# Eighteen orders of reading the streamed operand, one for each wide block, in a kernel of linear attention and a softplus feed-forward layer

## The chip, the cores and the metric

The kernel runs on one core of one Trainium2 chip. Time is device time in microseconds (us) of one launch. The time before is the median of three runs. The profile is of one further execution, recorded by the hardware profiler.

## What is computed

```
# q, k, v: (8, 8, 576, 64); g_norm: (64,)
kv  = einsum('bhsd,bhse->bhde', k, v)
out = einsum('bhsd,bhde->bhse', q, kv)
rms = sqrt(mean(out * out, axis=-1, keepdims=True) + 1e-06)
x   = (out / rms * g_norm).transpose(0, 2, 1, 3).reshape(4608, 512)
# moe_w_in: (512, 2048); moe_w_out: (2048, 512)
h = x @ w_in
g = maximum(h, 0.0) + log1p(exp(-abs(h)))
result = g @ w_out                  # (4608, 512), float32
```

## The kernel before

Nearly all the work is the two large products of the feed-forward layer. Each of their operands is split into three parts of a reduced 32-bit type, and each product is three matrix products, of part 0 with part 0, 1 with 1 and 2 with 2, summed in PSUM. So one logical product of a 128 x 128 weight piece with a block of columns is three matmuls.

There are three phases over the hidden width of 2048, which is cut into 16 chunks of 128.

- Phase 0 also does the attention. It goes over the 4608 tokens in twelve blocks of 384 (`n`), with hidden chunks 0 to 3 for the first four blocks and 0 to 5 for the rest. `step` has `mm1` (L863: 384 streamed columns, read in order, 12 matmuls) and `mm2` (L870: 512 streamed columns, read in order, 3 matmuls a tile of 128 tokens).
- Phases 1 and 2 go over the tokens in nine wide blocks of 512 (`n` from 0 to 8), and take the remaining hidden chunks two at a time: a pair `p` is chunks 2p and 2p + 1. `PAIRS` (L251) gives the pairs of each block: three in every block of phase 1, and in phase 2 three in the first three blocks and two in the last six. `STEPS` (L252) is the list of (phase, block, pair), 45 in all; `wide_step` (L1043) is one of them.

The first product of a wide step, `x @ w_in` for 256 hidden units and 512 tokens, uses a form with seven products of half size in place of eight. `units_of` (L958) prepares from the loaded tokens the seven streamed operands `u` (tiles `units`, `early` and `turned`), and `both` (L553) prepares the four combinations of the weights. `product(u, q)` (L1058) is one of the seven products: for the three parts `m` and the two halves `kd` of its contraction one matmul each, six in all. Its stationary operand is a 128 x 128 piece of the weights, its streamed operand is 256 columns (`HW`, half of `WIDE`) of `dst`, and its output is 256 columns of PSUM, quarter `q` of the step's two banks (`place(q)`). Streamed operand and output both go through `from_the_end` (L42), which cuts the 256 columns into 16 blocks of 16 and goes over the blocks from the last to the first, with the columns inside a block in ascending order. The output is taken in the same order as the operand, so each column arrives at its own place.

Between the products ScalarE copies a quarter to another (L1107, L1111) and VectorE adds (L1115); softplus is taken on ScalarE (L1093 and `x2`, `x4`, `xd_` in `wide_step`), the result is split again (L1123, L1126, L1129), and `mm2` (L1136) multiplies it with `w_out`: for two chunks and four tiles of 128 tokens three matmuls each, 24 a step, with 512 streamed columns read in ascending order. `leave` (L912) takes the sums out of PSUM.

The order in which every engine issues its instructions is written by `Plan.order` (L95), a list scheduler that runs when the program is built. It is given an estimated duration and a due position for each task; a whole product of six matmuls is one task on the PE queue with 710 ns (L1074). With this, products of one step, `mm2` of the step before and the loads of later blocks are interleaved. The order is not affected by how a matmul's operands are addressed.

Of the kernel before, what the change touches and what calls it, by code (L numbers as in the profile page):

```python
# [18 lines left out]
P = 128  # L19
# [19 lines left out]
    return x.rearrange(f"r ({' '.join(names)}) -> r {' '.join(names)}", **dict(zip(names, shape[1:])))  # L39


def from_the_end(x):  # L42

    return x.rearrange("p (b w) -> p b w", w=16)[:, ::-1]


class Slot:
# [159 lines left out]
def kernel(  # L207
# [24 lines left out]
    nc = tc.nc  # L232
# [17 lines left out]
    n_wide = n_tokens // WIDE  # L250
# [127 lines left out]
    def halves(src, e):  # L378

        return src[e * NP:(e + 1) * NP].rearrange("p s d -> s p d")  # L380
# [662 lines left out]
    def wide_step(k):  # L1043
        ph, n, p = STEPS[k]
        ab, gv = slot("ab"), slot("gvp")
        b = starts[k]
# [6 lines left out]
        def place(q):  # L1053
            return ab.tile[:, q // 2, q % 2 * HW:(q % 2 + 1) * HW]
# [3 lines left out]
        def product(u, q):  # L1058
            f, i = PRODUCTS[u]
            w = forms[p][f].tile  # L1060
            dst, v = unit_slots[ph, n, u]
            for m in range(3):
                for kd in range(2):
                    at = i * 2 * P + kd * P
                    nc.tensor.matmul(from_the_end(place(q)), lhsT=w[:, m, at:at + P],  # L1065
                                     rhs=from_the_end(dst.tile[:, m, v, kd] if u < 6 else dst.tile[:, m, kd]),
                                     start=(u == 0 and not m and not kd), stop=(m == 2 and kd == 1), skip_group_check=True)

        def multiply(u, q, after, pos, take=(), follows=None):
            f = PRODUCTS[u][0]  # L1070
            give = [unit_slots[ph, n, u][0]] if last else []
            if final and u in (2, 3, 5, 6):
                give.append(forms[p][f])
            return add("PE", 710, lambda: product(u, q), unit_done[ph, n, u] + forms_done[p][f] + list(after), pos, take, give,  # L1074
                       follows=follows)
# [19 lines left out]
        def begin():  # L1095
            new(ab, None)
            product(0, X)
# [168 lines left out]
```

## Time and profile before

| | us |
|---|---|
| median of three runs | 866.85 |
| lowest, highest | 865.42, 867.55 |
| the profiled execution's own time | 868.08 |
| its span, first to last instruction | 866.2 |
| granted TensorE clock, mean | 0.998 of full |
| TensorE busy | 851.7 |
| VectorE busy | 704.5 |
| ScalarE busy | 520.8 |

TensorE's instructions by line, from the groups of the profile (a line's groups by source tile are added):

| line | what | matmuls | streamed columns |
|---|---|---|---|
| L863 | first product, phase 0 | 768 | 384 |
| L870 | second product, phase 0 | 576 | 512 |
| L1065 | the seven products, phases 1 and 2 | 2016 | 256 |
| L1136 | second product, phases 1 and 2 | 1152 | 512 |

The profile gives a matmul as an interval from its start to a modelled end. Matmuls are pipelined, so these intervals overlap and their mean length is more than the distance between two starts. The chain of waits follows the work that ended last back to its start, and its pieces of one line in a row give that distance: length over count. The first instruction of L1065 starts at 340.6 us, in the last stretch of phase 0, and the last at about 854; phases 1 and 2 fill the rest of the span. The last block ends with 39 matmuls of L1136 (8.92 us from 853.52), a scaling of the last tile and its store.

### The profile page before, as it was taken

How to read it: one execution, taken by the hardware profiler on the slowest of the kernel's cores; microseconds unless marked ns; L12 is line 12 of the kernel's file. 1: busy time of each engine (PE TensorE's matmuls, PEld its weight loads, DVE VectorE, ACT ScalarE, POOL GpSimd, SP SyncE). 2: the span in 40 equal slices, each digit the busy share in tenths (PEclk: the TensorE clock that was granted, in tenths of full speed). 3: DMA queues.
4: the chain of work that ended last, by engine and by line, in shares of the span. 5: the costliest groups of instructions: out<-in, count | busy, mean ns of one | idle time of the engine just before them, and what ended most of it. 6: DMA issues, size and time to landing. Idle time of an engine off the chain costs nothing.

```text
span 866.2 us, 17080 instructions
## 1 busy us (share of the span) xinstructions
PE 851.7 (98%) x6464; PEld 758.6 (88%) x6464; DVE 704.5 (81%) x995; ACT 520.8 (60%) x980; POOL 76.1 (9%) x79
## 2 busy tenths in 40 slices
PE   7899999999999999999999999999999999999998
PEld 5678888989898899998999998998999899999996
DVE  7888898888788889798888788878788766788873
ACT  5766565445344567776667665655868555566654
POOL 0351123111113300000000000000000000000000
PEclk9999999999999999999999999999999999999999
DMA  9998997778774655436645546645354653787764
GB/s 273 278 218 216 285 259 227 188 250 215 206 186 119 194 157 180 143 113 198 211 155 161 167 152 203 193 154 185 122 191 139 233 166 100 238 240 237 247 189 128
DMA packets 239778, 167.07 MB, mean 193 GB/s; under 512 B 106320, under 2 KB 198736, under 8 KB 239696
## 3 DMA queue, kind: packets, MB, share of 16 engines
q1 hardware_dynamic: 239392, 165.86, 64.8%
q8 instruction: 50, 0.82, 0.4%
q14 instruction: 32, 0.26, 0.1%
q10 hardware_dynamic: 304, 0.13, 0.1%
HBM read 112.98 MB, written 52.95 MB: 192 GB/s over the span
## 4 chain that ended last, share of the span: by engine, by line
PE 93%; DMA 3%; DVE 2%; ACT 1%; POOL 1%; SPq 0%; issue 0%; DVEq 0%; ACTq 0%
PE banks L1136 30%; PE banks L1065 28%; PE banks L870 15%; PE banks L863 15%; PE banks L720 2%; PE banks L696 2%; DMA loads<-in_v_dram 1%; DMA raw<-in_moe_w_in_dram 1%; PE banks L738 0%; PE banks L1230 0%; POOL roots L728 0%; DVE half L732 0%; SPq L766 0%; DVE units L643 0%; ACT w L802 0%
## 5 line engine op out<-in xcount | busy, mean ns | idle before, releaser
L1136 PE MATMUL banks<-pieces,gv 128*128 128x512 f32 x768 | 238.1, 391 | 0.0
L1136 PE MATMUL banks<-pieces,g_False 128*128 128x512 f32 x384 | 150.6, 392 | 0.0
L1136 PEld LDWEIGHTS banks<-pieces,gv 128*128 128x128 f32 x768 | 132.6, 188 | 17.8
L863 PE MATMUL banks<-units,pieces 128*128 128x384 f32 x768 | 145.4, 337 | 0.0
L870 PE MATMUL banks<-pieces,gv 128*128 128x512 f32 x576 | 144.9, 396 | 0.0
L863 PEld LDWEIGHTS banks<-units,pieces 128*128 128x128 f32 x768 | 135.5, 188 | 4.9
L870 PEld LDWEIGHTS banks<-pieces,gv 128*128 128x128 f32 x576 | 106.1, 188 | 20.4
L1065 PEld LDWEIGHTS banks<-units,pieces 128*128 128x128 f32 x840 | 112.0, 188 | 6.6 <-ACT banks L1111 0.4
L1065 PE MATMUL banks<-units,pieces 128*128 128x256 f32 x840 | 116.4, 282 | 0.0
L885 ACT ACTIVATE half<-banks 128x384 f32<-128x384 f32 x64 | 31.5, 491 | 97.8 <-PE banks L863 97.7
L1126 DVE TENSOR_TENSOR gv<-g_True,gv 128x1024 fp32r<-128x1024 f32 x47 | 57.5, 1223 | 37.2 <-ACT gv L1123 37.2
L1136 PEld LDWEIGHTS banks<-pieces,g_False 128*128 128x128 f32 x384 | 71.9, 187 | 16.5
L1065 PEld LDWEIGHTS banks<-units,w 128*128 128x128 f32 x504 | 67.3, 188 | 3.8 <-ACT banks L1111 0.2
L1065 PE MATMUL banks<-units,w 128*128 128x256 f32 x504 | 70.3, 282 | 0.0
L728 POOL TENSOR_TENSOR roots<-roots,half 128x8 f32<-128x8 f32 x36 | 62.0, 1722 | 3.0
L1129 DVE SCALAR_TENSOR_TENSOR g_False<-gv 128x1024 fp32r<-128x1024 f32 x47 | 57.6, 1225 | 1.5
L1028 DVE TENSOR_TENSOR units<-loads,units 128x1024 fp32r<-128x1024 f32 x42 | 51.2, 1219 | 6.3 <-ACT units L1025 6.3
L1115 DVE TENSOR_TENSOR g_True<-banks,g_True 128x512 f32<-128x512 f32 x48 | 33.1, 691 | 28.4 <-PE banks L1065 23.1
L1093 ACT ACTIVATE g_True<-banks 128x256 f32<-128x256 f32 x96 | 36.7, 383 | 31.8 <-PE banks L1065 31.2
L930 ACT ACTIVATE m<-banks 128x512 f32<-128x512 f32 x72 | 42.1, 596 | 18.5 <-PE banks L1136 12.9
L1031 DVE SCALAR_TENSOR_TENSOR units<-units 128x1024 fp32r<-128x1024 f32 x42 | 51.4, 1223 | 1.8
L1025 ACT ACTIVATE units<-loads 128x1024 fp32r<-128x1024 f32 x42 | 44.4, 1057 | 13.4 <-PE banks L1065 10.4
(115 smaller groups left out, 1252.0 us busy)
## 6 DMA issues: line engine op xcount, KB each, us to landing
loads<-x SPq DMA_DIRECT2D x180, 128.0 KB, 2.7
part<-m SPq DMA_DIRECT2D x72, 256.0 KB, 2.8
m<-part SPq DMA_DIRECT2D x72, 256.0 KB, 3.3
loads<-form SPq DMA_DIRECT2D x45, 256.0 KB, 3.2
form<-loads SPq DMA_DIRECT2D x36, 256.0 KB, 2.9
raw<-in_moe_w_in_dram SPq DMA_DIRECT2D x16, 512.0 KB, 4.6
loads<-in_k_dram SPq DMA_DIRECT2D x32, 256.0 KB, 4.3
loads<-in_v_dram SPq DMA_DIRECT2D x32, 256.0 KB, 4.6
```

What stands on the lines that cost most here:

```text
L728: nc.gpsimd.tensor_tensor(out=r.tile, in0=r.tile, in1=half, op=ALU.pow)
L863: nc.tensor.matmul(hp, lhsT=w_in.tile[:, i, kd * P:(kd + 1) * P], rhs=xv.tile[:, i, kd], start=(m == 0), stop=(m == 3 * KD - 1))
L870: nc.tensor.matmul(mine[i].tile, lhsT=gv.tile[:, m, i * P:(i + 1) * P], rhs=w_out.tile[:, m], start=(c == cs[0] and m == 0), stop=(c == cs ...
L930: a = add("ACT", 690 if ph == LAST else 600, lambda: nc.scalar.activation(new(ot, [P, d_model]), bank.tile, func=AF.Copy, scale=scale if p ...
L1025: nc.scalar.activation(part_of(0, F32R), xl.tile if m > 1 else xl.tile[:, 0], func=AF.Copy, scale=DOWN)
L1028: nc.vector.tensor_tensor(out=part_of(1, F32R), in0=xl.tile if m > 1 else xl.tile[:, 0], in1=part_of(0), op=ALU.subtract)
L1031: nc.vector.scalar_tensor_tensor(out=part_of(2, F32R), in0=part_of(1), scalar=-RADIX, in1=part_of(0), op0=ALU.mult, op1=ALU.add)
L1065: nc.tensor.matmul(from_the_end(place(q)), lhsT=w[:, m, at:at + P], rhs=from_the_end(dst.tile[:, m, v, kd] if u < 6 else dst.tile[:, m, kd ...
L1093: nc.scalar.activation(dst, src, func=AF.Softplus, scale=1.0 + E)
L1126: nc.vector.tensor_tensor(out=gvt(1, F32R), in0=gt(), in1=gvt(0), op=ALU.subtract)
L1129: nc.vector.scalar_tensor_tensor(out=gt(F32R), in0=gvt(1), scalar=-RADIX, in1=gvt(0), op0=ALU.mult, op1=ALU.add)
L1136: nc.tensor.matmul(mine[i].tile, lhsT=(gvt(m, F32R) if m < 2 else gt(F32R))[:, c, i * P:(i + 1) * P], rhs=outs[c].tile[:, m], start=fresh ...
```

## The change: one order for each wide block

`from_the_end` is replaced by `in_order(x, k)`, which has eighteen ways to go over the 256 columns. `k` is 0 to 8 for the wide blocks of phase 1 and 9 to 17 for those of phase 2. All matmuls of the seven products of a block use its order, for the streamed operand and for the output alike, so the same numbers arrive at the same places.

```diff
-def from_the_end(x):
-
-    return x.rearrange("p (b w) -> p b w", w=16)[:, ::-1]
+def in_order(x, k):
+
+    def blocks(w):
+        return x.rearrange("p (b w) -> p b w", w=w)
+
+    def halves(w):
+        return x.rearrange("p (e j w) -> p j e w", e=2, w=w)
+
+    def quarters(w):
+        return x.rearrange("p (e j w) -> p j e w", e=4, w=w)
+
+    def inside(e, w):
+        return x.rearrange("p (b e w) -> p b e w", e=e, w=w)
+
+    return [lambda: x,
+            lambda: blocks(16)[:, ::-1],
+            lambda: blocks(8)[:, ::-1],
+            lambda: blocks(4)[:, ::-1],
+            lambda: blocks(32)[:, ::-1],
+            lambda: blocks(64)[:, ::-1],
+            lambda: blocks(2)[:, ::-1],
+            lambda: halves(16)[:, ::-1],
+            lambda: inside(8, 16)[:, :, ::-1],
+            lambda: inside(4, 16)[:, :, ::-1],
+            lambda: quarters(16)[:, ::-1, ::-1],
+            lambda: quarters(4),
+            lambda: quarters(8),
+            lambda: halves(16)[:, ::-1, ::-1],
+            lambda: inside(2, 16)[:, :, ::-1],
+            lambda: inside(4, 8)[:, :, ::-1],
+            lambda: inside(4, 4)[:, :, ::-1],
+            lambda: x[:, ::-1]][k]()
...
-                    nc.tensor.matmul(from_the_end(place(q)), lhsT=w[:, m, at:at + P],
-                                     rhs=from_the_end(dst.tile[:, m, v, kd] if u < 6 else dst.tile[:, m, kd]),
+                    k = n_wide * (ph - 1) + n
+                    nc.tensor.matmul(in_order(place(q), k), lhsT=w[:, m, at:at + P],
+                                     rhs=in_order(dst.tile[:, m, v, kd] if u < 6 else dst.tile[:, m, kd], k),
```

In words, by the number of the order:

- 0: ascending, one run of 256 columns.
- 1: blocks of 16 columns from the last to the first, as before. 2, 3, 4, 5 and 6: the same with blocks of 8, 4, 32, 64 and 2.
- 7: the halves in turn, a run of 16 from each, from the end of both. 13: the same, with the upper half first.
- 8, 9 and 14: groups of 8, 4 and 2 runs of 16; the groups ascend, and the runs inside a group go backward. 15 and 16: groups of 4 runs of 8 and of 4 columns, in the same way.
- 10: the quarters in turn, a run of 16 from each, from the end, with the last quarter first. 11 and 12: the quarters in turn, runs of 4 and of 8, ascending.
- 17: every single column from the last to the first.

## The prediction

> **What bounds the kernel now.** I read the page first, for the busy shares, then the chain of waits, for who sets the end, then the waits of the changed line, and last the chain in order of time, for the pitch of its matmuls.
>
> ```profile
> span 866.2 us, 17080 instructions
> PE 851.7 (98%) x6464; PEld 758.6 (88%) x6464; DVE 704.5 (81%) x995; ACT 520.8 (60%) x980; POOL 76.1 (9%) x79
> ...
> PE 93%; DMA 3%; DVE 2%; ACT 1%; POOL 1%; SPq 0%; issue 0%; DVEq 0%; ACTq 0%
> ...
> L1065 PE MATMUL banks<-units,pieces 128*128 128x256 f32 x840 | 116.4, 282 | 0.0
> ```
>
> TensorE is busy for 98% of the span and holds 93% of the chain that ended last. The row of L1065 (one of its five, by source tile) shows no idle time before its matmuls. Its mean of 282 ns is one matmul from its start to its modelled end; consecutive ones overlap, so it is not what one costs. The instructions of L1065 and their waits say how much slack stands in front of them:
>
> ```profile
> its engine sat idle before it (us, times) until:
>   ACT banks L1111: 0.6, 3
> ```
>
> 0.6 us in 2016 matmuls: a nanosecond more on one of them is a nanosecond more of span, and a nanosecond less is one less, as long as VectorE (339.7 us busy in the 420 us from 380 to 800) and ScalarE (262.5 us) keep up. The price of one matmul is its pitch, which the chain in order of time gives, as the length of an unbroken run over its count:
>
> ```profile
> 130.28 4.12 PE banks L870 x18
> 138.86 4.19 PE banks L863 x24
> ...
> 383.74 2.75 PE banks L1136 x12
> ...
> 485.61 2.84 PE banks L1065 x24
> ```
>
> L863 streams 384 columns: 4.19 / 24 = 174.6 ns. L870 and L1136 stream 512: 4.12 / 18 = 228.9 and 2.75 / 12 = 229.2 ns. L1065 streams 256 in reversed blocks of sixteen: 2.84 / 24 = 118.3 ns, and the same 2.84 stands in run after run, over several wide blocks. L863, L870 and L1136 read straight ahead.
>
> **The change.** Nothing is added or removed: the same 2016 matmuls, with the same loads, waits and buffers; no DMA, queue or wait moves. What changes is the order in which 256 columns are read from SBUF and, in the same order, accumulated in PSUM. Each wide block has one order: 3 steps of 7 products of 6 matmuls make 126 for the nine blocks of phase 1 and the first three of phase 2; the last six have 2 steps, 84. 12 x 126 + 6 x 84 = 2016. Order 1 is today's, so 1890 matmuls change.
>
> No row shows a 256-column matmul of L1065 read in another order. The bounds come from the neighbours. *Straight ahead:* the line through 384 and 512 columns falls by 229.2 - 174.6 = 54.6 ns for 128 columns and gives 120.0 ns at 256, 1.7 above today's. Pure proportion, with no fixed part, gives 174.6 x 256 / 384 = 116.4, 1.9 below. So any order of long runs lies, as a change, between -1.9 x 1890 = -3.6 us and +1.7 x 1890 = +3.2 us. *Orders of short runs* (two columns in order 6, single columns read backward in order 17, four in 3, 11 and 16): at worst each column takes two slots, and a 256-column matmul costs what a 512-column one does: 229.2 - 118.3 = +110.9 ns. At best nothing.
>
> I take these values. Orders 2 to 5, 7, 10 and 13 begin at or near the far end, as today's does: 0. Order 0 (126), 11 (126) and 12 (84) go upward: the full 1.7 ns, 336 x 1.7 = 0.57 us. Orders 8, 9, 14, 15 and 16 go backward only inside groups that go upward: half, (2 x 126 + 3 x 84) x 0.85 = 0.43 us. Orders 6 and 17: 0, because they still use every column of each small neighbourhood one after the other, and because today's fifteen jumps show no price: 118.3 lies below the 120.0 of the straight line. That is the weakest step; its upper ends are 126 x 110.9 = 14.0 us (order 6) and 84 x 110.9 = 9.3 us (order 17). Sum: +1.0 us.
>
> One more row makes small prices small: a weight load of L1065 takes 188 ns and runs beside the matmuls, with the weight row busy 379.5 of 420 us. No row tells whether the stream or the load sets the pitch of 118.3; if it is the load, an order a little slower is hidden behind it.
>
> A block that gets slower makes nothing else late: ScalarE already waits for L1065 (50.0 us at the copy of L1111, 31.2 at the softplus of L1093), and those waits only grow; SP's loads come earlier relative to their use. A block that gets faster meets the few waits on ScalarE first.
>
> The profiled execution took 868.08 us around its span of 866.2; the median of the three runs is 866.85. The sum is a difference, so on the profiled execution it gives 869.1 and on the median **867.9 us**, which I forecast.
>
> [...]
>
> **The rivals.**
>
> *Single columns backward are slow (slower).* [...] 84 x 110.9 = +9.3 us on top of the 1.0: 866.85 + 10.3 = 877.2. [...] Against it: the same neighbours are still read one right after another. [...]
>
> *Runs of two are slow as well.* Then order 6 costs 14.0 us: with order 17, 891.1; alone, 881.9. For it: 127 jumps against today's 15. [...]
>
> *Each jump has a small price.* Taking today's 118.3 as 116.4 plus fifteen jumps, a jump costs (118.3 - 116.4) / 15 = 0.127 ns. Orders differ from today's by -15 jumps (0), +16 (2, 12, 15), +48 (3, 11, 16), -8 (4), -12 (5) and +112 (6): over the 126 of the long blocks these add up to 126 x (-15 + 16 + 48 - 8 - 12 + 112 + 48) = 23814 jumps, over the 84 of the short ones 84 x (16 + 16 + 48) = 6720, together 3.9 us; with 240 more in order 17, 20160 jumps, 6.4 us. Time: 870.8 to 873.3. Against it: the straight line, by which jumps cost nothing.
>
> *Runs of four are slow too.* Orders 3, 11 and 16, 336 x 110.9 = +37.2 us: 928.4 with the others. Today's row says nothing of runs this short.
>
> *Today's order is a poor one (faster).* If the proportion holds and most orders reach 116.4, up to -3.6 us: 863.2, more likely half, 865.0. For it: proportion is the only lower bound there is. Against it: it leaves no fixed part, while the two widths show none either way.
>
> *The order does nothing at all,* since the weight load sets the pitch: 866.85. It is one case with the forecast.
>
> **How the numbers follow.** Chances: forecast 0.38, single columns slow 0.24, two columns slow 0.10 (0.03 of it without order 17), jumps priced 0.14, runs of four slow 0.06, faster 0.08. What a measurement of this kernel can tell from no change is about 0.3%, 2.6 us: 864.25 to 869.45. The forecast's own range, with the bounds of the long runs, is 863.5 to 870.1; of its 0.38, 0.30 fall within 0.3%, 0.06 above, 0.02 below. Jumps: 0.11 slower, 0.03 within. Faster: 0.06 and 0.02 within. Three cases of slow short runs: all 0.40 slower. Together faster 0.08, within 0.35, slower 0.57: the likeliest single case is within the bound, yet the slower cases together weigh more. The range has to take in the single-column case with the error of the long runs (877.2 + 3) and order 6 alone (881.9): 863.5 to 883.0. Left out are both short-run orders slow (0.07), runs of four (0.06) and the far end of faster (0.03), 0.16.
>
> **What would show it.** In the chain in order of time, runs of L1065 x24 of 2.8 to 2.9 us in every wide block say the forecast is right. A step now takes 42 x 118.3 + 24 x 229.2 ns = 10.5 us, the three-step block 31.4 and the last 20.9. If order 17 is slow, the last block takes 30.3 us and its runs of six 1.37 instead of 0.71; if order 6 is, the seventh block takes 45.4. If jumps are priced, the run of 24 grows in step with the count of jumps, most in order 6 (118.3 + 14.2 = 132.5 ns). Straight-ahead block 0 at 2.88 us for 24 would confirm the line, at 2.79 the proportion. A wait of L1065 above a few us in total, or other groups of instructions growing, would refute the claim that only the pitch matters. The forecast is wrong if any single block is over 2.6 us longer.

## The result, and the profile after

The changed kernel takes 871.24 us (median of four runs, 870.83 to 872.0) against 866.7 before (four runs, 865.42 to 867.55): 4.5 us more, ratio 1.0055 with a 95% interval of 1.0037 to 1.0072.

From the page of the changed kernel, where L1095 is the line of the seven products and L1166 that of the second product:

```profile
span 868.9 us, 17077 instructions
PE 855.7 (98%) x6464; PEld 762.4 (88%) x6464; DVE 704.8 (81%) x995; ACT 522.2 (60%) x980; POOL 76.0 (9%) x79
...
PE 94%; DVE 2%; DMA 2%; ACT 1%; POOL 1%; issue 0%; SPq 0%; DVEq 0%; ACTq 0%
...
L1095 PE MATMUL banks<-units,pieces 128*128 128x256 f32 x840 | 118.5, 284 | 0.0
```

TensorE still sets the end and still hardly waits before the changed line. In the list of L1095 with its waits, its engine sits idle before it for the same 0.6 us as before, and the others wait a little longer for it (VectorE's addition 28.8 us where it was 23.1):

```profile
  ACT banks L1141: 0.6, 3
...
  DVE g_True L1145: 28.8, 32
```

The span is only 2.7 us longer. That hides part of the loss: in this execution phase 0 went faster, and L1095 starts at 337.7 us where it started at 340.6. From there to the end it is 531.2 us against 525.6, 5.6 more.

The chain in order of time (start, length, line and count) shows where they lie:

```profile
359.09 8.63 PE banks L1095 x72
...
451.70 2.84 PE banks L1095 x24
...
525.17 2.87 PE banks L1095 x24
...
574.12 4.35 PE banks L1095 x36
...
609.36 2.84 PE banks L1095 x24
...
704.57 3.23 PE banks L1095 x24
...
822.70 3.20 PE banks L1095 x24
...
845.12 2.13 PE banks L1095 x18
```

These are the blocks of orders 0, 3, 5, 7, 8, 11, 16 and 17. Length over count gives the pitch, the distance from one matmul's start to the next: 119.9, 118.3, 119.6, 120.8, 118.3, 134.6, 133.3 and 118.3 ns. Two orders stand out, 11 and 16, and neither is the one with the smallest pieces: single columns backward (17) cost nothing.

For all orders I took the distance of consecutive starts in the trace, a mean over the products of a block without its first and last two, in the same block before and after (ns):

| order | levels (outer, middle, run) | before | after | difference |
|---|---|---|---|---|
| 0 | straight | 118.3 | 119.7 | +1.4 |
| 1 | 16 blocks of 16 backward | 118.8 | 118.8 | 0 |
| 2 | 32 blocks of 8 backward | 118.2 | 119.7 | +1.4 |
| 3 | 64 blocks of 4 backward | 118.0 | 118.2 | +0.1 |
| 4 | 8 blocks of 32 backward | 118.0 | 118.9 | +0.8 |
| 5 | 4 blocks of 64 backward | 117.9 | 119.3 | +1.4 |
| 6 | 128 blocks of 2 backward | 118.3 | 118.1 | -0.2 |
| 7 | halves in turn [8, 2, 16] | 118.3 | 120.4 | +2.1 |
| 8, 9 | groups of 128 and 64, [2, 8, 16] and [4, 4, 16] | 118.3 | 118.3 | 0 |
| 10 | quarters in turn [4, 4, 16] | 119.0 | 120.5 | +1.6 |
| 11 | quarters in turn [16, 4, 4] | 117.9 | 135.1 | +17.2 |
| 12 | quarters in turn [8, 4, 8] | 118.1 | 119.2 | +1.1 |
| 13 | halves in turn [8, 2, 16] | 118.0 | 120.2 | +2.2 |
| 14 | groups of 32, [8, 2, 16] | 118.1 | 119.8 | +1.7 |
| 15 | groups of 32, [8, 4, 8] | 118.1 | 119.5 | +1.4 |
| 16 | groups of 16, [16, 4, 4] | 118.1 | 132.8 | +14.7 |
| 17 | single columns backward | 118.2 | 118.1 | -0.2 |

All distances of the line add up to 243.3 us, against 238.3. Orders 11 and 16 hold 126 x 17.2 + 84 x 14.7 ns = 3.4 us of these 5.0, ten of the others nearly all of the remaining 1.6. The second product adds 0.6 (264.5 against 263.9), and 5.0 + 0.6 is the 5.6 us above.

### The profile page after: what moved, and what is told of

Read it like the earlier page. It is cut to its first block, busy times and chain, and to the rows that moved or that the text cites. A ratio compares the mean times of both kernels' runs of the same rounds, so it can differ in the third digit from the quotient of the medians.

```text
span 868.9 us, 17077 instructions
## 1 busy us (share of the span) xinstructions
PE 855.7 (98%) x6464; PEld 762.4 (88%) x6464; DVE 704.8 (81%) x995; ACT 522.2 (60%) x980; POOL 76.0 (9%) x79
## 4 chain that ended last, share of the span: by engine, by line
PE 94%; DVE 2%; DMA 2%; ACT 1%; POOL 1%; issue 0%; SPq 0%; DVEq 0%; ACTq 0%
PE banks L1166 30%; PE banks L1095 28%; PE banks L899 16%; PE banks L892 15%; PE banks L749 2%; PE banks L725 2%; DMA raw<-in_moe_w_in_dram 1%; DMA loads<-in_v_dram 1%; PE banks L767 0%; POOL roots L757 0%; PE banks L1260 0%; DVE half L761 0%; SPq L795 0%; DVE units L672 0%; ACT w L831 0%
## 5 line engine op out<-in xcount | busy, mean ns | idle before, releaser
L1166 PE MATMUL banks<-pieces,gv 128*128 128x512 f32 x768 | 239.1, 392 | 0.0
L1166 PE MATMUL banks<-pieces,g_False 128*128 128x512 f32 x384 | 150.2, 391 | 0.0
L1166 PEld LDWEIGHTS banks<-pieces,gv 128*128 128x128 f32 x768 | 133.2, 188 | 18.2
L1095 PEld LDWEIGHTS banks<-units,pieces 128*128 128x128 f32 x840 | 113.8, 189 | 6.8 <-ACT banks L1141 0.4
L1095 PE MATMUL banks<-units,pieces 128*128 128x256 f32 x840 | 118.5, 284 | 0.0
L1166 PEld LDWEIGHTS banks<-pieces,g_False 128*128 128x128 f32 x384 | 72.1, 188 | 16.4
L1095 PEld LDWEIGHTS banks<-units,w 128*128 128x128 f32 x504 | 68.4, 189 | 3.9 <-ACT banks L1141 0.2
L1095 PE MATMUL banks<-units,w 128*128 128x256 f32 x504 | 71.6, 284 | 0.0
L1145 DVE TENSOR_TENSOR g_True<-banks,g_True 128x512 f32<-128x512 f32 x48 | 33.1, 691 | 31.5 <-PE banks L1095 28.8
```

The costliest lines, as they stand in the source:

```text
L1095: nc.tensor.matmul(in_order(place(q), k), lhsT=w[:, m, at:at + P], rhs=in_order(dst.tile[:, m, v, kd] if u < 6 else dst.tile[:, m, kd], k) ...
L1166: nc.tensor.matmul(mine[i].tile, lhsT=(gvt(m, F32R) if m < 2 else gt(F32R))[:, c, i * P:(i + 1) * P], rhs=outs[c].tile[:, m], start=fresh ...
```

## The experiments

Twelve kernels ran. Pitches below are taken as in the table, each from the one profiled execution of its kernel; "median" marks the median in place of the mean.

**Does the price belong to the order or to the block?** The same eighteen orders, moved by nine blocks (the list in short, not the code itself):

```diff
-    return [orders 0 .. 17][k]()
+    return [orders 9 .. 17, 0 .. 8][k]()
```

> The eighteen orders of the change, each moved to the wide block nine places on: orders 9 to 17 stand in phase 1, orders 0 to 8 in phase 2. Theory (the price belongs to the order): order 11 (quarters in turn, runs of four) costs 135 ns a matmul in its new block, the third of phase 1 (runs of 24 in the chain of 3.2 us), order 16 costs 133 in the eighth of phase 1, and the two blocks that were slow fall to 118 to 120 ns (2.83 to 2.88 us). Orders 3, 6, 8, 9 and 17 stay at 118.2, orders 0, 2, 4, 5, 7, 10, 13, 14 and 15 at 119 to 120. Rival (the price belongs to the block: its tiles, its neighbours on the other engines): the third and eighth blocks of phase 2 stay at 135 and 133, whatever order they have.

Order 11 in the third block of phase 1 has 135.3 ns, order 16 in the eighth 133.0; the blocks that were slow have 119.7 (order 2) and 120.1 (order 7). The others keep their pitches to within 0.8 ns. From the chain, order 11 in its new block:

```profile
418.32 3.25 PE banks L1095 x24
```

3.25 / 24 = 135.4 ns. The price goes with the order, as the theory had it.

**What in the order?** Eighteen others, most of them ascending groups with the runs inside a group backward:

```diff
+            lambda: inside(2, 4)[:, :, ::-1],
+            lambda: inside(8, 4)[:, :, ::-1],
...
+            lambda: inside(2, 8)[:, :, ::-1],
+            lambda: inside(8, 8)[:, :, ::-1],
+            lambda: inside(8, 2)[:, :, ::-1],
...
+            lambda: inside(4, 2)[:, :, ::-1],
```

> Eighteen other orders, one for each block in the order of blocks; an order is given as its levels [outer, middle, run]. 0: [32, 2, 4], 1: [8, 8, 4], 2: [4, 16, 4], 3: [2, 32, 4], 4: [16, 2, 8], 5: [4, 8, 8], 6: [16, 8, 2], 7: [4, 32, 2], 8: [64, 2, 2], all with ascending groups and the runs inside a group backward; 9: [32, 2, 4] as halves in turn; 10: [8, 8, 4] as eighths in turn; 11: quarters in turn, the last first, [16, 4, 4]; 12: [32, 4, 2] as 0 to 8; 13: two levels, [64, 4], single columns backward in ascending groups of four; 14 and 15: orders 11 and 16 of the change, [16, 4, 4]; 16: the order of before; 17: sixteenths in turn, [4, 16, 4]. Theory A (each step of the outer level costs about one ns when the run is short): +31 ns for the 32 outer steps of 0 and 9, +15 for 6, 11, 14 and 15, +7 for 1 and 10, +3 for 2 and 17, +1 for 3, +63 for 8, and 4 and 5 near +1 to +2, 13 nothing. Rival B (any three-level order with runs of four or fewer pays the same): +15 for all of 0 to 3, 6 to 12 and 17. Rival C (each upward jump pays, whatever the levels): as A for three levels, and +63 for 13.

All three fail. The lines are from the chain of this kernel: the fifth block (groups of 16 as two runs of eight) and the first block of the short ones (groups of eight as four pairs):

```profile
484.43 3.20 PE banks L1095 x24
...
743.65 2.72 PE banks L1095 x24
```

133.3 and 113.3 ns. Theory A had groups of 16 in runs of two at +15, which came, but groups of eight in runs of four at +31, and these are the fast ones; B gave one price to all. For orders that go backward inside ascending groups, the large differences go with the number of columns in a group, and not with its runs or its count of jumps. In ns, with the first table's orders:

| columns in a group | pitch, by run length |
|---|---|
| 4 | 119.0 (2), 119.4 (1) |
| 8 | 113.3 (2); 113.3 (4, median; its block is the first, with a mean of 116.4) |
| 16 | 132.8 (2), 132.8 (4), 132.8 (8) |
| 32 | 119.2 (4, median), 119.5 (8), 119.8 (16) |
| 64 | 118.4 (2), 118.1 (4), 119.7 (8), 118.3 (16) |
| 128 | 118.2 (4), 118.3 (16) |
| 256 | 118.1 (1), 118.1 (2), 118.2 (4), 119.7 (8), 118.1 (16), 118.9 (32), 119.3 (64) |

Interleaved stretches have prices of their own: halves in runs of four 126.4 ns, quarters 135.1 either way round, eighths 120.2 (median), sixteenths 114.1. Two things follow. A group of exactly 16 columns is slow whether it is cut in twos, fours or eights; and some orders are *faster* than the one of before. Two things do not: the differences of one to two ns inside a row of the table go with neither the group nor the run, and order 11 has no backward group at all. Its price goes with the interleaving, and no rule found here covers it together with order 16.

**Reading or writing?** The streamed operand and the output were given different orders:

```diff
-                    nc.tensor.matmul(in_order(place(q), k), lhsT=w[:, m, at:at + P],
+                    nc.tensor.matmul(in_order(place(q), k, True), lhsT=w[:, m, at:at + P],
```

> Read order and written order are given apart, so that a block's hidden columns are permuted and its rows of the result land in other places. Blocks 0 and 1: order 16 read and written straight, and the reverse; 2 and 3: the same with order 11; 4, 12: 16 and 11 on both sides; 5: straight on both; 6, 7, 8: order 1 read, written, both; 9, 10, 11: order 7 read, written, both; 13, 14: order 3 read, written; 15, 16: order 17 read, written; 17: order 10 on both. Theory (the stream from SBUF pays): +13 to +17 ns over 118.2 in blocks 0 and 2, none in 1 and 3. Rival (PSUM pays, whose neighbours the writes break up): the reverse. Rival (the addresses are made one by one, on whichever side): +13 to +17 in all four and the same with both sides.

Order 16 read and written straight: 133.0 ns; straight read and written in order 16: 119.8. Order 11: 135.1 and 119.3. Both sides alike: 132.9 and 135.2. Orders 1, 3 and 17 show the same on the small scale: read 118.3, 118.1 and 118.1, written 119.4, 119.1 and 119.1, where straight on both sides has 119.3. The chain of this kernel, in the first (order 16 read), second (written) and third block (order 11 read):

```profile
360.52 9.60 PE banks L1114 x72
...
388.13 2.15 PE banks L1114 x18
...
420.08 3.25 PE banks L1114 x24
```

133.3, 119.4 and 135.4 ns. The price of orders 16 and 11 is one of reading, as the theory had it. Written orders had 119.1 to 119.8 ns with straight reading, where straight writing has 119.3, so here PSUM took them at the pace of a straight one. Order 7 alone does not separate: read 120.0, written 120.4, both 120.0, and the block in which it was written is that of order 10 in the first table, 119.0 before where the others have 117.9 to 118.8.

**How much of the loss is two orders?** Two complementary kernels: the change without orders 11 and 16, and these two alone.

```diff
-            lambda: quarters(4),
+            lambda: blocks(16)[:, ::-1],
...
-            lambda: inside(4, 4)[:, :, ::-1],
+            lambda: blocks(16)[:, ::-1],
```

> Orders 11 and 16 are replaced by the order of before in their two blocks; the other orders are those of the change. Theory (these two orders carry most of the loss): 126 x 17.0 + 84 x 14.8 ns = 3.4 us less than the 871.2 of the change, 867.8 to 868.0, ratio to before 1.001 to 1.002. Rival (the loss is spread over all orders, one to two ns each): 870.7 or more, ratio 1.0045 or more.

> The order of before in all blocks but two, which keep orders 11 and 16. Theory (these two orders carry most of the loss of the change): 126 x 17.0 + 84 x 14.8 ns = 3.4 us over before, 870.0, ratio 1.0039. Rival (they lose less in a kernel than their pitch says, as the 1.9 us between the change and the kernel without them suggests): 1.9 us, ratio 1.0022. Rival (none): 1.000.

Without them 869.31 us, ratio 1.0023 (1.0011 to 1.0035): 2.0 us over before by the ratio, 2.7 by the medians (866.6 beside it). Alone 869.74, ratio 1.0036 (1.0024 to 1.0048): 3.1 us by the ratio, 2.6 by the medians (867.16 beside it). The second agrees with the theory, and its trace has 241.7 us for the seven products (+3.4) and 264.0 for the second product (+0.1). The first came out 1.3 us above what I expected, between the theory and the rival. Its trace does not show this excess in the distances: the seven products take 239.9 us, the expected 3.4 less than in the change, and the second product 264.5, as in the change. What differs is phase 0, from which it begins the seven products at 339.4 us and the change at 337.7; whether that is more than chance isn't shown. 2.0 + 3.1 is 5.1, against 4.5 for both, or 4.8 by its ratio: within the intervals. By the traces the two orders carry 3.4 of the 5.6 us, three fifths of the loss; by the medians, taking them out of the change saved 1.9 us and putting them alone into the kernel before cost 2.6, of 4.5.

**Is pitch all that counts?** The fast order found above, in every block:

```diff
-    return x.rearrange("p (b w) -> p b w", w=16)[:, ::-1]
+    return x.rearrange("p (b e w) -> p b e w", e=4, w=2)[:, :, ::-1]
```

> All seven products of all wide blocks read and write in ascending groups of eight columns with the four pairs of a group backward (levels [32, 4, 2], 113.3 ns a matmul in one block of the second set of orders, the same in all six positions of a product). Theory (TensorE sets the end and its pitch is all that counts): 2016 x (118.2 - 113.3) = 9.9 us less than before, 856.7, ratio 0.9886; runs of 24 in the chain 2.72 us. Rival (other engines take over: ScalarE's copies and softplus between the products): the pitch falls, waits of TensorE appear, and less than half of it, over 861.7, is kept. Rival (that block was special): pitch 118, no change.

855.07 us, ratio 0.9864 (0.9845 to 0.9884): 11.5 us less than before by the medians (866.54 beside it), 11.8 by the ratio, and 16.2 less than the change. The chain:

```profile
512.07 2.72 PE banks L1065 x24
514.78 2.72 PE banks L1136 x12
...
593.71 2.87 PE banks L1065 x24
```

The seven products stand at 2.72 / 24 = 113.3 ns in block after block, with few exceptions (the last line has 119.6), and add up to 229.4 us, 8.9 less than before. The second product, which was not touched, went from 2.75 to 2.72 us for twelve, 261.2 us in all, 2.7 less. The sum, 11.6, is what the times show; the theory had 9.9, without the part of the second product. TensorE does not begin to wait (0.6 us before this line, as before), so nothing is given back.

**The same order on the longer matmuls.**

```diff
-                nc.tensor.matmul(mine[i].tile, lhsT=(gvt(m, F32R) if m < 2 else gt(F32R))[:, c, i * P:(i + 1) * P], rhs=outs[c].tile[:, m],
+                nc.tensor.matmul(in_eights(mine[i].tile), lhsT=(gvt(m, F32R) if m < 2 else gt(F32R))[:, c, i * P:(i + 1) * P], rhs=in_eights(outs[c].tile[:, m]),
```

and the same on both lines of phase 0.

> The same groups of eight on the other three lines too: the first product of phase 0 (384 columns, 768 matmuls), and the second products (512 columns, 576 and 1152). Theory (the price lies in the stream's reads, whatever the length): at the same ns for each matmul 2496 x 4.9 = 12.2 us less than with the seven products alone, 844.5; at the same ns for each column 768 x 7.35 + 1728 x 9.8 = 22.6 us less, 834.1. Runs in the chain: x12 of the second product 2.63 to 2.69 us, x24 of the first 4.01 to 4.07. Rival (only the short matmuls, next to whose stream the weight load takes nearly as long, pay for it): no more than with the seven products alone, 856.7.

> The seven products all in groups of eight; the other three lines in one order for each block. First and second product of phase 0, blocks 0 to 11: straight, 1, [.., 4, 2], [.., 2, 4], 16, 3, sixteenths, eighths in runs of 4, [.., 2, 2], [.., 2, 8], 15, 17. Second product of phases 1 and 2: the same twelve in blocks 0 to 11, then 12: thirty-seconds in runs of 4, 13: sixteenths in runs of 8, 14: sixteenths in runs of 2, 15: [.., 8, 1], 16: halves in runs of 4, 17: quarters in runs of 4. Theory (what counts is how a group lies in a stretch of 16 columns): the same ranking as at 256 columns: groups of 8 best, groups of 16 worst, over 20 ns above straight at 512 columns. Rival (long matmuls hide it): all within 2 ns of 229 and 174.5.

Everywhere: 870.43 us, ratio 1.0045 (1.003 to 1.006), worse than all expectations. Against the kernel with the seven products alone every part lost: the seven products 5.6 us (235.0), the second product 5.6 (266.7), the two lines of phase 0 2.9 (139.6) and 1.3 (137.4). Together that is 15.4 us, which is the difference of the times. The chain shows both pitches of the seven products in one kernel, and the slower second product:

```profile
528.81 2.88 PE banks L1065 x24
531.68 2.79 PE banks L1136 x12
...
602.02 2.73 PE banks L1065 x24
604.75 2.78 PE banks L1136 x12
```

The kernel with an order for each block gave, as medians, for 512 columns in phases 1 and 2: straight 227, order 1 233, groups of eight 231, groups of 16 266 (runs of four) and 267 (runs of eight), single columns 233, thirty-seconds in turn in runs of four 224, but sixteenths in runs of four 247, quarters 269 and eighths 277. For 384 columns groups of 16 have 200 where straight has 174.5, groups of eight 180, and sixteenths in runs of four 227. Of the backward groups those of 16 are the worst at all three lengths; of all orders they are not, since interleaved ones cost more. That groups of eight are best holds at 256 columns only. From 256 to 384 to 512 columns, groups of 16 rise from 132.8 to 200 to 266: 0.52 ns a column, where straight reading in the kernel before rises by (228.9 - 174.6) / 128 = 0.42. Read in groups of 16, the stream was slower at all three lengths.

**Can the two gains be added?** The groups of eight for the seven products, and the best of the 512-column orders for the second product:

```diff
+    return x.rearrange("p (e j w) -> p j e w", e=32, w=4)
```

> The seven products in ascending groups of eight with the pairs backward, as in the run that did so, and the second product of phases 1 and 2 reads and writes its 512 columns as thirty-seconds in turn in runs of four, whose block had 224.9 ns a matmul where straight reading had 226.7. Theory: 1152 x 1.8 ns = 2.1 us less than with the groups of eight alone (855.1): 853.0, ratio 0.984. Rival (the gain of that block is of the block): 855.1. Rival (its reads make the seven products' pitch worse, as neighbours): over 856.

862.0 us, ratio 0.994 (0.9927 to 0.9954): the third expectation. The second product fell (260.0 us, 1.2 less, where 2.1 was hoped for), but the seven products, with the same order, rose by 8.7 to 238.1. The chain shows how, product by product, in one stretch:

```profile
503.37 2.88 PE banks L1070 x24
506.26 2.70 PE banks L1141 x12
...
537.94 0.73 PE banks L1070 x6
...
541.42 3.42 PE banks L1070 x30
...
546.86 0.69 PE banks L1070 x6
```

A run of 24 has 120.0 ns, the run of 30 in the next block 114.0. Here the same instruction with the same operand order has one of two pitches, about 120 and 114 ns, and most products of six stay in one of them.

**Is it the weight load's reads?** Two kernels with the weight tiles 32 and 64 bytes further from the streamed tiles, and one that loads half the weight columns, and so writes half the rows of PSUM and leaves half of the hidden units out:

```diff
-    SHIFT = 64
+    SHIFT = 72
...
-    SHIFT = 64
+    SHIFT = 80
...
-                    nc.tensor.matmul(in_order(place(q), k), lhsT=w[:, m, at:at + P],
+                    nc.tensor.matmul(in_order(place(q)[:P // 2], k), lhsT=w[:, m, at:at + P // 2],
```

> All weight tiles stand 32 bytes further on, relative to the tiles that the seven products stream (the gap between them has 72 words in place of 64). Orders by block: 0: 0, 1: 16, 2: [32, 4, 2], 3: sixteenths in turn [4, 16, 4], 4: 1, 5: 11, 6: 2, 7: 17, 8: 9, 9: 7, 10: 12, 11: [32, 2, 4], 12: 14, 13: 15, 14: [8, 8, 4], 15: 0, 16: 16, 17: [32, 4, 2]. Theory (reads of the stream collide with those of the weight load, so the place of one relative to the other counts): the pitches change by more than 3 ns in several orders; 16 leaves 133, or [32, 4, 2] leaves 113.3. [...]

> As the run with the weight tiles 32 bytes further on and the same orders by block, with 64 bytes in place of 32. Theory (collisions of the two reads, with a pattern that repeats every 64 bytes): the pitches come back to those of the old distance within 0.5 ns: [32, 4, 2] 113.3, [32, 2, 4] 113.3, order 1 118.2, order 2 119.6, order 9 118.3, order 0 119.4. Rival (the pattern is longer): they differ from both distances, and [32, 4, 2] stays over 115. Orders 16 and 11 stay at 133 and 135 in each case.

> The seven products load only the first 64 of each 128 weight columns, so that half of the hidden units isn't computed; orders by block as in the run with the weight tiles 32 bytes further on, tiles at the old distance. Theory (part of the pitch is collision with the weight load's reads): with half of these reads gone the orders that stood at 118 to 120 (0, 1, 2, 17, 9, 7, 12, 14, 15) fall by 2 ns or more, towards 113, and move together; [32, 4, 2] and [32, 2, 4] change by less than 2 ns; 16 and 11, whose own reads are slow, stay over 130. Rival (the weight load is not involved): all as at full width within 1 ns. Rival (the weight load sets the pitch of all fast orders): 113.3 falls too, by 3 ns or more.

| order | old distance | 32 bytes | 64 bytes | half the weight columns |
|---|---|---|---|---|
| groups of 8, pairs [32, 4, 2] | 113.3 | 118.9 | 118.2 | 118.1 |
| groups of 8, fours [32, 2, 4] | 113.3 (median) | 119.0 | 118.0 | 118.1 |
| 0, straight | 119.7 | 118.4 | 117.0 | 114.7 |
| 1, before | 118.3 | 119.1 | 118.0 | 117.8 |
| 2, blocks of 8 | 119.7 | 117.9 | 119.2 | 118.0 |
| sixteenths | 114.1 | 114.7 | 114.4 | 114.5 |
| 16 | 132.8 | 132.8 | 132.7 | 132.9 |
| 11 | 135.1 | 135.7 | 135.8 | 133.9 |

The chain of the kernel with half the weight columns, in its blocks of orders 0, 16 and [32, 4, 2]:

```profile
359.63 8.27 PE banks L1095 x72
...
400.22 3.20 PE banks L1095 x24
...
418.47 2.83 PE banks L1095 x24
```

114.9, 133.3 and 117.9 ns. Two prices come apart. The price of orders 16 and 11 stays at 132.7 to 132.9 and 133.9 to 135.8 ns at all three places of the weights and with half of their columns loaded: with the experiment on reading and writing (133.0 and 135.1 ns read, 119.8 and 119.3 written), it is put down to the stream's own reading. The range from 113 to 120 does move: 32 bytes take the groups of eight from 113.3 to 119, and the kernel with half the weight columns takes the straight order from 119.7 to 114.7. The first kernel agrees in this with its theory; the other two fail theirs. 64 bytes do not bring the old pitches back, which is the rival there. With half the columns, of the nine orders that were to fall by 2 ns or more only 0 and 7 did (order 7 from 120.4 to 118.2), and the groups of eight, which were to stay, rose by 4.8.

That the weight load's reads do this isn't shown. The shift moves the operands of the second product against each other as well (its distances went from 264.5 us in the change to 268.2 with 32 bytes), and in the experiment before, its change of order came with 8.7 us more of the seven products. The halved kernel also writes half the rows.

## Why the prediction was right and where it failed

The time lies in the range (863.5 to 883.0) and the ratio in the class with the highest chance, slower at 0.57. The forecast itself, 867.9, was too low by 3.3 us, and the case that came true was none of those written down. So the class and the range were luck. The time lies above the forecast's own range (863.5 to 870.1), and the rest, up to 883.0, was there for single columns and runs of two. The 0.57 was added up from the upper end of the forecast, priced jumps and three cases of slow short runs, and what made the kernel slower is mainly two orders that the sum had at 0.29 us. By the prediction's own sign, runs of 24 of 2.8 to 2.9 us in every wide block, the forecast fails in the blocks of orders 11 and 16, with 3.23 and 3.20.

- **TensorE's pitch goes to the end one for one: shown, to within about 1 us.** The kernel in groups of eight lost 11.6 us of distances and 11.5 of time; the kernel with that order everywhere took 15.4 more of one and 15.4 more of the other; the change itself has 5.6 and 4.5. That nothing but the changed line's pitch moves did not hold: the second product took 0.6 us more in the change and 2.7 less in groups of eight.
- **Straight ahead at 120.0 ns: right.** Block 0 has 119.7, and straight reading elsewhere 119.1 to 119.8 as long as the tiles and loads are those of the change. The lower bound by proportion, 116.4, was not a bound: groups of eight have 113.3.
- **Orders 6 and 17 at nothing: right**, 118.1 ns each, though called the weakest step.
- **Orders 11 and 16 at 1.7 and 0.85 ns: this step failed.** They cost 17.2 and 14.7 ns, 3.4 us where I had 0.29. I sorted orders by where they begin and by the length of their runs; the runs with twos and ones were priced as the risk, and the sum took these two as long runs. For order 16 what counts is its group: 16 columns read backward cost 132.8 ns in runs of two, four or eight alike, and order 3, with the same runs of four over all 256 columns, costs nothing. For order 11 it is the interleaving: with the same ascending runs of four, halves have 126.4 ns, quarters 135.1 and sixteenths 114.1. Why is open.
- **Orders 2, 5, 7, 10 and 13 at nothing: too low**, by 1.4 to 2.2 ns. With 14 and 15, which cost 1.7 and 1.4 where half of 1.7 was taken, they make up most of the rest of the error.
- **The price of each jump:** the time fell into this rival's span (870.8 to 873.3), but the mechanism did not decide. Order 6 with 127 jumps has 118.1 ns, where 132.5 was due.
- **Runs of two and runs of four slow:** refuted by order 6 and order 3 (118.1 and 118.2 ns, where 229.2 was due). Two of the three orders of this last rival are slow, but by 17.2 and 14.7 ns and not 110.9.
- **Single columns backward slow:** refuted by order 17, which has 118.1 ns where 229.2 was due, and 119.1 where it was written only (straight 119.3). The 110.9 ns of this rival, two slots for a column, was an estimate of mine that no run shows at 256 columns; the highest pitch given here for 256 columns is 135.8 ns.
- **The weight load may set the pitch:** refuted in the form given, since with the same loads (188 ns each, before and in groups of eight) the pitch is 118.3 and 113.3 ns. Whether the loads take part in the range from 113 to 120 is not shown: moving them (groups of eight from 113.3 to 118.9 ns) and halving them (straight from 119.7 to 114.7) changed it, and each changed something else with it.
- **Today's order is a poor one:** true, but by orders that the change does not contain.

What stays open: why a product of six matmuls settles at 113.3 or 120.0 ns, why the second product's order has a say in which, why a group of 16 columns is slow at all three lengths (132.8, 200 and 266 ns), and why four interleaved quarters are. The pitch changed with the tiles' places (113.3 to 118.9 ns for the groups of eight, 32 bytes further on) and with the neighbouring instructions (2.7 us on a line that was not touched); no run shows the path.

## What to carry to other kernels

Where TensorE is the bound, the order in which a matmul reads its streamed operand is a free parameter, worth 1.4% here, and a diagnostic kernel with one order for each block prices eighteen of them in one profile. A pitch found in one block has to be tried in the whole kernel, with its neighbours: the best order for one line cost 5.6 us on the next, and an order for the next cost the first 8.7. The size of an order's pieces did not tell its price: look at the stretch within which it turns back (113.3 ns in groups of eight, 132.8 in groups of 16) and at how many stretches it interleaves (135.1 for quarters in runs of four, 114.1 for sixteenths), and measure.

## What was not expected of the hardware

- Reading 256 columns one by one from the end costs the same as the best of the orders of the change (118.1 ns), and writing PSUM backward in single columns, in runs of four and in the two slow orders costs nothing (119.1 to 119.8 ns with straight reading, where straight writing has 119.3).
- Ascending groups of exactly 16 columns (64 bytes) read backward take 0.52 ns a column at 256, 384 and 512 columns, whether cut in pairs, fours or eights (pairs at 256 only).
- Sixteenths of 512 columns in turn, in runs of two, have a median of 450 ns where straight reading has 227, half the pace; sixteenths in runs of four have 247 and thirty-seconds in runs of four 224. From the chain of the kernel with an order for each block, in the block of runs of two:

```profile
819.18 5.41 PE banks L1152 x12
```
- The pitch of a matmul changed with the matmuls around it: the second product, whose order was untouched, took 261.2 us, 2.7 less than before, when the seven products changed theirs.
